# Second expert products with w2 as weights: 256 tokens moved, the result turned and brought back through DRAM

## The chip, the cores and the metric

The kernel runs on one core of a Trainium2 chip. The metric is the device time of one execution in microseconds. The kernel before was run three times; the median is 2457.13 us (2457.12 to 2459.16).

Engines are named as in the profile: PE is TensorE's matmuls and PEld its weight loads, DVE is VectorE, ACT ScalarE, POOL GpSimd, SP SyncE. A name with a q, such as SPq, is the engine's instruction queue, which also issues DMA transfers. All data are 32-bit floats.

## The reference

```python
# attention: u, v (8, 2496, 256), z (8, 2496, 64)
scores = (1.0 / S) * np.matmul(z, z.transpose(0, 2, 1))
attn = np.maximum(scores, 0.0) ** 2
x = (u * np.matmul(attn, v)).reshape(19968, 256)
# experts: w1 (8, 256, 1024), w2 (8, 1024, 256)
expert_idx = token_ids * np.int64(2654435761) % np.int64(8)
for e in range(8):
    mask = expert_idx == e
    h = np.maximum(x[mask] @ w1[e], 0.0)
    out[mask] = h @ w2[e]
```

## The kernel before

The first part computes the attention, and beside it sorts the tokens by expert: each row of x is scattered to a slot in DRAM (`x_slots`), so that tokens of one expert lie together. The second part works through the slots in 40 big blocks (`NL`) of 512 tokens, each with one expert, and one small block of 128.

A big block has two layers. Both are done by a scheme of Strassen's kind: each operand is split into four quarters, and seven products of sums of quarters take the place of eight. `products` (L929) writes down the order of the seven (1, 6, 7, 5, 2, 3, 4) and what is added to what, and yields after each. Products 1 and 5 stay in a PSUM bank of the tag "held" (two banks), since products 2 and 3 are added to them in place; 6, 7 and 4 pass through the tag "other". The second layer has only one "other" bank, so product 7 can't be written before VectorE has added product 6 to product 1 (`ro`, L935), and product 4 not before product 7 is read.

- `up_big` (L955) is the first layer: w1 quarters are the weights, 256 tokens are moved at a time, and the hidden features lie on the partitions. It goes through the seven products twice, two slices of hidden features at a time: 14 steps, called U. A step is four matmuls of 256 columns. A 32-bit matmul shows as two records in the profile, so a step has 8 records.
- `down_big` (L987) is the second layer: the hidden values of 128 tokens are the weights, and 128 output features of w2 are moved, so that the result has tokens on the partitions, as rows. It has seven steps, called D, of 8 matmuls of 128 columns (16 records) each. VectorE and ScalarE put the results into `o_sb` (two buffers); when the rows of two 128-token tiles are complete, `store` (L921) has GpSimd scatter them to the output by an indirect DMA.

What is done when is written out by hand: `tc.manual_schedule()` keeps every engine's instructions in the order in which the program issues them. The outer loop (L1056) has 41 iterations. Iteration i takes the U steps of block i, the D steps of block i-1, and the two X steps of block i+1 (`turn_x`, L742: X1 turns the loaded tokens by VectorE's transposes of 32x32 squares, L752; X2 makes their sums, L757 to L760). A string gives the order:

```python
    ORDER = {"first": "UUUUGUUUGUUUUUUU", "second": "DUDUDUUDUUDUU" "XUxUDUXUDUUUU",
             "other": "UuUDUuUXDUdUDU" "UDUDUxUDUXUDU", "end": "DDDDDDDd"}
```

Small letters belong to the small block and are empty until the last but one iteration. An iteration of the kind "other" is therefore U1 U2 D1 U3 U4 X1 D2 U5 U6 D3 U7 U8 D4 U9 D5 U10 U11 D6 U12 X2 U13 D7 U14; D1, D2, D3 are products 1, 6, 7, and D7 is product 4.

At the end of iteration i, SyncE's queue gets the loads in this order:

```python
        for j in at(i + 2):
            load_x(j)
        for m in range(2):
            for j in at(i + 2 - m):
                load_w(j, m)
```

`load_x` (L735) loads a block's tokens into `xq` by four DMAs of 128 KB, in pieces of 256 B; it has two buffers, and the buffer for block i+2 is free once block i is turned, in iteration i-1. `load_w` (L763) loads w1 or w2 with the quarter sums prepared earlier (1792 KB each, in pieces of 14336 B per partition); w1 of block i+2 needs the buffer of block i, free after the last U step of iteration i. So SyncE's queue waits at the weights until an iteration's end, issues them, and then issues the next block's `xq` at once, an iteration early.

The quarters of w2 and their sums are prepared in the attention part (`prepare`, L678) and addressed by `w2_block` (L714). With the output features split in two, a quarter's columns are either contiguous halves or, after the change, every second column.

The attention part has transfers of the same form as the ones of the change: after each tile of queries, four DMAs write `x_sb` to DRAM (`put`, L364; 4 x 128 KB in pieces of 256 B), and the rows are fetched again (L372, L223; pieces of 1 KB).

Of the kernel before, what the change touches and what calls it, by code (L numbers as in the profile page):

```python
# [10 lines left out]
F32 = mybir.dt.float32  # L11
# [13 lines left out]
def kernel(  # L25
# [10 lines left out]
    nc = tc.nc  # L36

    B, S, D = u.shape
    K = z.shape[-1]
    N = B * S  # L40
    E, _, F = moe_w1.shape
# [3 lines left out]
    P = 128  # L45
    L = 32
    DP = D // P
    FP = F // P
# [6 lines left out]
    BLK = 512  # L55
    TB = BLK // P
    NL = E * -(-N // (E * BLK))
# [84 lines left out]
    FQ = FP // 2  # L142
# [565 lines left out]
            nc.gpsimd.dma_start(out=w_dram[e, m], in_=w[:].rearrange("p i f -> p (i f)"))  # L708


    def w1_block(w, i):
        return w[:, i]

    def w2_block(w, i):  # L714
        if i < 4:
            return w[:, 0:4].rearrange("p i f -> p (i f)").rearrange("p (c f i d) -> p c i f d", c=2, f=FQ, i=2)[:, i // 2, i % 2]
        return w[:, i].rearrange("p (f d) -> p f d", f=FQ)


# [2 lines left out]
    w1, w2, xq, xT, hid = {}, {}, {}, {}, {}  # L722

    def big(j):
        return j < NL
# [6 lines left out]
    def half(j):  # L732
        return len(slot_tiles(j)) * P // 2
# [29 lines left out]
    def load_w(j, m):  # L763

        e = nc.sync.value_load(eb_i[0:1, j:j + 1], min_val=0, max_val=E - 1)
        if big(j):
            w = (w2pool if m else wpool).tile([P, 7, HF], F32, name="w")
            nc.sync.dma_start(w[:].rearrange("p i f -> p (i f)"), w_dram[ds(e, 1), m].rearrange("one p f -> (one p) f"))
        elif m == 0:
            w = w2pool.tile([P, DP, F], F32, name="w1s")  # L770
            nc.sync.dma_start(
                w[:], moe_w1[ds(e, 1)].rearrange("one d f -> (one d) f").rearrange("(c p) f -> p c f", p=P))
        else:
            w = w2pool.tile([P, FP, D], F32, name="w2s")
            nc.sync.dma_start(
                w[:], moe_w2[ds(e, 1)].rearrange("one f d -> (one f) d").rearrange("(c p) d -> p c d", p=P))
        (w1, w2)[m][j] = w
# [52 lines left out]
    for i, (b, g, s) in enumerate(steps):  # L830
# [54 lines left out]
        elif is_routed:  # L885
            if fetched and i >= fetched[0][0] + (5 if i < len(steps) - NT else 2):
                rows = fetched.pop(0)[1]
# [33 lines left out]
    def store(j, t, o):  # L921
        col = slot_tiles(j)[t]
        st = nc.gpsimd.indirect_dma_start(  # L923
            out=out[:], out_offset=bass.IndirectOffsetOnAxis(ap=idx[:, col:col + 1], axis=0),
            in_=o, in_offset=None, bounds_check=N - 1, oob_is_err=False)
        tc.declare_no_dep(st.ins, group="rows", reason="each token has its own row")
        tc.add_to_no_dep_group("rows", st.ins)

    def products(made, p1, u, c11, c12, c21, c22, done):  # L929


        ps1 = made(1, None)
        nc.scalar.copy(p1, ps1)
        yield
        nc.vector.tensor_add(u, p1, made(6, None))  # L935
        yield
        ps7 = made(7, None)
        yield
        ps5 = made(5, None)
        nc.vector.tensor_add(c21, u, ps7)  # L940
        nc.vector.tensor_add(c22, c21, ps5)  # L941
        done(c22, 1, 1)
        yield
        made(2, ps1)
        done(c11, 0, 0, ps1)
        yield
        made(3, ps5)
        nc.vector.tensor_add(c12, u, ps5)
        done(c12, 0, 1)
        yield  # L950
        nc.vector.tensor_sub(c21, c21, made(4, None))
        done(c21, 1, 0)
        yield
# [30 lines left out]
            nc.vector.tensor_sub(x21, x11, x21)  # L984
            nc.vector.tensor_sub(s4, x12, s2)

    def down_big(j):  # L987
        h, sums = hid[j]
        n = half(j) // P
        x11, x12, x21, x22 = (h[:, k, i] for i in range(2) for k in range(2))  # L990
        s1, s2, s4 = (sums[:, i] for i in range(3))
        take = {1: (x11, 0), 2: (x12, 2), 3: (s4, 3), 4: (x22, 6), 5: (s1, 4), 6: (s2, 5), 7: (x21, 1)}

        def made(m, ps):
            first = ps is None
            if first:
                held = m in (1, 5)
                ps = down_ps.tile([P, 2, P], F32, name="o_ps", tag="held" if held else "other", bufs=2 if held else 1)[:, 0:n]
            x, k = take[m]
            for t in range(n):  # L1000
                for f in range(FQ):
                    nc.tensor.matmul(ps[:, t], x[:, f, ts(t, P)], w2_block(w2[j], k)[:, f], start=first and t == 0 and f == 0,  # L1002
                                     stop=f == FQ - 1, skip_group_check=True)
            return ps
        r = rpool.tile([P, 2, 2, P], F32, name="ro")[:, :, 0:n]
        o = rpool.tile([P, TB, D], F32, name="o_sb")
        c = lambda i, k: o[:, ts(i, n), ts(k, P)]

        def done(x, i, k, ps=None):
            if ps is not None:  # L1010
                nc.scalar.copy(x, ps)
            elif i != k:
                for t in range(i * n, i * n + n):
                    store(j, t, o[:, t, :])
        yield from products(made, r[:, 0], r[:, 1], c(0, 0), c(0, 1), c(1, 0), c(1, 1), done)

    def up_small(j):
        x = xT[j][0]
# [37 lines left out]
    for i in range(NL + 1):  # L1056
        parts = {}
        for j in at(i):
            parts["U" if big(j) else "u"] = (up_big if big(j) else up_small)(j)
        for j in at(i - 1):  # L1060
            parts["D" if big(j) else "d"] = (down_big if big(j) else down_small)(j)
        for j in at(i + 1):
            if i:
                parts["X" if big(j) else "x"] = turn_x(j)
        if i == 0:
            x_sb = late.tile([P, 2, 2, D], F32, name="x_row")
            parts["G"] = gate_at_once(*done, x_sb, lambda: down_ps.tile([P, 2, D], F32, name="g_ps", tag="held", bufs=2))
        for p in ORDER["first" if i == 0 else "second" if i == 1 else "end" if i == NL else "other"]:
            next(parts.get(p, iter(())), None)
        for p in parts.values():  # L1070
            assert next(p, None) is None and next(p, "end") == "end"
        if i == 0:
            for k in range(4):
                sort(*done[:2], x_sb, k)
            closing["late"].close()
            w2pool = pool("w2pool", 2, reuse_waits="tile")
            load_w(0, 1)
# [5 lines that stand above are left out]
# [4 lines left out]
    n_others = nc.values_load(others_i[0:1, 0:1], min_val=0, max_val=NR - SMALLS)  # L1087
    with tc.For_i(0, n_others, 1) as n:
        e = nc.sync.value_load(eb_i[0:1, ds(n + NL + SMALLS, 1)], min_val=0, max_val=E - 1)
        w1s = w2pool.tile([P, DP, F], F32, name="w1s")  # L1090
        nc.sync.dma_start(w1s[:], moe_w1[ds(e, 1)].rearrange("one d f -> (one d) f").rearrange("(c p) f -> p c f", p=P))
        w2s = w2pool.tile([P, FP, D], F32, name="w2s")
        nc.sync.dma_start(w2s[:], moe_w2[ds(e, 1)].rearrange("one f d -> (one f) d").rearrange("(c p) d -> p c d", p=P))
        x_in = gpool.tile([P, P // L, DP, L], F32, name="xqs")
        src = x_dram[ds((n + NL * TB + SMALLS) * P, P), :].rearrange("(j r) (i e) -> i r j e", r=L, e=DL)
        for i in range(P // L):
            nc.sync.dma_start(out=x_in[ts(i, L)].rearrange("r j h k -> r j (h k)"), in_=src[i])
        to = rpool.tile([P, 1], I32, name="to")
        nc.sync.dma_start(out=to[:], in_=slot_dram[:].rearrange("(p c) -> p c", p=P)[:, ds(n + NL * TB + SMALLS, 1)])
        x = gpool.tile([P, 1, DP, P], F32, name="xTs")  # L1100
        nc.vector.transpose(x[:, 0].rearrange("p h (j r) -> p j h r", r=L), x_in[:])
        h = hpool.tile([P, FP, P], F32, name="h1")
        for f in range(0, FP, 4):
            ps = down_ps.tile([P, 4, P], F32, name="h_ps", tag="any")
            for i in range(4):
                for c in range(DP):
                    nc.tensor.matmul(ps[:, i, :], w1s[:, c, ts(f + i, P)], x[:, 0, c], start=(c == 0), stop=(c == DP - 1))
            nc.vector.tensor_scalar_max(h[:, f:f + 4], ps[:], 0.0)
        ps = down_ps.tile([P, D], F32, name="o_ps", tag="any")
        for f in range(FP):  # L1110
            nc.tensor.matmul(ps[:], h[:, f], w2s[:, f, :], start=(f == 0), stop=(f == FP - 1))
        o = rpool.tile([P, D], F32, name="o1")
        nc.scalar.copy(o[:], ps[:])
        nc.gpsimd.indirect_dma_start(
            out=out[:], out_offset=bass.IndirectOffsetOnAxis(ap=to[:, 0:1], axis=0),
            in_=o[:], in_offset=None, bounds_check=N - 1, oob_is_err=False)
# [28 lines left out]
```

## Time and profile before

| what | value |
|---|---|
| median of 3 runs | 2457.13 us |
| the profiled execution's own time | 2461.1 us |
| its span, first to last instruction | 2459.3 us |
| mean granted TensorE clock | 0.998 |
| HBM read, written | 332.83 MB, 179.81 MB |
| matmul and weight-load records of L1002 (D steps) | 4480 each |
| mean duration of a record: 128 columns (L1002), 256 columns (L971) | 275 ns, 380 ns |

[...] The busy share of an engine is over the whole span; the two parts have different limits. The expert stage runs from about 1450 us to the end, one block in 24.59 us.

### The profile page before, as it was taken

What the parts mean: (1) busy time and instruction counts of PE and PEld (TensorE: products, weight loads), DVE (VectorE), ACT (ScalarE), POOL (GpSimd) and SP (SyncE); (2) the same over time, 40 slices, a digit from 0 to 9 for tenths busy, and PEclk for the clock granted to TensorE, in tenths of its full rate; (3) what the DMA queues carried; (4) which work ended last, traced back from release to release, by engine and by line L of the source; (5) the groups of instructions that cost most, each with busy time, mean ns of one, the idle gap of its engine ahead of it and who ended that gap; (6) DMA issues with size and microseconds to landing.
All of it is one profiled execution on the core that took longest, in us unless ns stands there. A gap on an engine that the chain in (4) does not pass through costs nothing.

```text
span 2459.3 us, 36675 instructions
## 1 busy us (share of the span) xinstructions
PE 2435.6 (99%) x13351; PEld 2075.4 (84%) x13351; DVE 1767.7 (72%) x3655; ACT 728.5 (30%) x1210; POOL 570.9 (23%) x547
## 2 busy tenths in 40 slices
PE   8999999999999999999999999999999999999998
PEld 6787787787787787787787789999999999999997
DVE  7778778868868769778778666666666666666663
ACT  4324314324224224224233212222222222222221
POOL 0002013423524424423321021111111111121112
PEclk9999999999999999999999999999999999999999
DMA  7866667888888788878778686565656565656562
GB/s 150 202 201 188 163 191 235 241 270 249 249 257 254 253 244 254 253 217 248 259 214 248 196 236 192 186 199 187 198 188 197 188 197 187 197 187 199 187 208 73
DMA packets 412104, 518.94 MB, mean 211 GB/s; under 512 B 254252, under 2 KB 347261, under 8 KB 393488
## 3 DMA queue, kind: packets, MB, share of 16 engines
q1 hardware_dynamic: 350704, 326.23, 47.4%
q10 hardware_dynamic: 32448, 97.86, 12.0%
q0 software_dynamic: 28768, 92.49, 10.4%
q8 instruction: 105, 1.72, 0.3%
q14 instruction: 79, 0.65, 0.1%
HBM read 332.83 MB, written 179.81 MB: 208 GB/s over the span
## 4 chain that ended last, share of the span: by engine, by line
PE 94%; DMA 2%; issue 2%; DVE 1%; SPq 1%; ACT 0%; ACTq 0%; POOL 0%; another core or an unknown queue 0%; DVEq 0%; POOLq 0%
PE acc L326 45%; PE o_ps L1002 20%; PE h_ps L971 20%; PE s_ps L251 9%; DMA v_sb<-in_v_dram 1%; DMA zT<-zT 0%; DMA x<-x_sb 0%; SPq L303 0%; ACT a L255 0%; DMA a<-scores 0%; DVE t L275 0%; DMA zn<-in_z_dram 0%; POOL out_dram L923 0%; PE h_ps L1025 0%; SPq L364 0%
## 5 line engine op out<-in xcount | busy, mean ns | idle before, releaser
L255 ACT ACTIVATE a<-s_ps 128x512 f32<-128x512 f32 (+1 forms) x480 | 246.7, 599 | 703.4 <-PE s_ps L251 586.8
L326 PE MATMUL acc<-t,vc 128*128 128x256 f32 (+3 forms) x1600 | 402.2, 373 | 0.0
L326 PEld LDWEIGHTS acc<-a,v_sb 128*128 128x128 f32 (+1 forms) x1600 | 293.2, 190 | 119.1 <-issue 53.1
L326 PE MATMUL acc<-a,v_sb 128*128 128x256 f32 (+3 forms) x1600 | 382.7, 382 | 0.1
L326 PE MATMUL acc<-t,v_sb 128*128 128x256 f32 (+3 forms) x1600 | 369.7, 373 | 0.0
L923 POOL DMA_INDIRECT out_dram<-o_sb,idx x160 | 162.3, 1014 | 822.6 <-issue 774.8
L411 POOL DMA_INDIRECT x_slots<-x_row,row x160 | 192.8, 1205 | 685.6 <-DVE x_row L389 510.8
L326 PEld LDWEIGHTS acc<-t,vc 128*128 128x128 f32 (+1 forms) x1600 | 303.5, 190 | 33.6
L326 PEld LDWEIGHTS acc<-t,v_sb 128*128 128x128 f32 (+1 forms) x1600 | 303.4, 190 | 33.7
L1002 PEld LDWEIGHTS o_ps<-w,h 128*128 128x128 f32 x2560 | 311.4, 192 | 9.1 <-DVE ro L935 0.8
L971 PE MATMUL h_ps<-xs,w 128*128 128x256 f32 x1280 | 316.6, 380 | 0.0
L1002 PE MATMUL o_ps<-w,h 128*128 128x128 f32 x2560 | 312.2, 275 | 0.6 <-DVE ro L935 0.6
L275 DVE TENSOR_TENSOR t<-a 128x512 f32<-128x512 f32 (+1 forms) x200 | 134.3, 671 | 206.2 <-ACT a L264 147.5
L978 ACT ACTIVATE h<-h 128x512 f32<-128x512 f32 x240 | 151.4, 631 | 413.4 <-DVE h L941 177.6
L251 PE MATMUL s_ps<-zT 64*128 64x512 f32 (+1 forms) x960 | 242.8, 619 | 9.7 <-DVE zT L186 6.9
L971 PEld LDWEIGHTS h_ps<-xs,w 128*128 128x128 f32 x1280 | 228.8, 191 | 23.1
L1002 PEld LDWEIGHTS o_ps<-w,hs 128*128 128x128 f32 x1920 | 233.1, 192 | 6.1
L971 PE MATMUL h_ps<-xT,w 128*128 128x256 f32 x960 | 234.5, 380 | 3.1 <-DVE h L941 3.1
L1002 PE MATMUL o_ps<-w,hs 128*128 128x128 f32 x1920 | 233.8, 275 | 0.0
L291 DVE STREAM_TRANSPOSE mirror<-a 128x256 f32<-128x256 f32 x640 | 217.7, 406 | 0.6 <-DMA scores<-mirror 0.6
L662 POOL DMA_INDIRECT slot_tokens<-token,addr x160 | 170.6, 1066 | 134.1 <-DVE addr L650 85.7
L326 PE MATMUL acc<-a,vc 128*128 128x256 f32 (+3 forms) x800 | 201.1, 373 | 0.0
(169 smaller groups left out, 2384.0 us busy)
## 6 DMA issues: line engine op xcount, KB each, us to landing
w<-w_blocks SPq DMA_DIRECT2D x80, 1792.0 KB
scores<-mirror SPq DMA_DIRECT2D x192, 256.0 KB
a<-scores ACTq DMA_DIRECT2D x48, 1024.0 KB
scores<-mirror SPq DMA_DIRECT2D x224, 128.0 KB
a<-scores ACTq DMA_DIRECT2D x32, 896.0 KB
w_blocks<-w POOLq DMA_DIRECT2D x16, 1792.0 KB
xq<-x_slots SPq DMA_DIRECT2D x160, 128.0 KB
u_sb<-in_u_dram SPq DMA_DIRECT2D x72, 256.0 KB
```

The source lines that it names most:

```text
L251: nc.tensor.matmul(flat(ps)[:, 0:2 * w].rearrange("p (q c) -> p q c", q=2), tile_of_keys(b, h, s, j), q_h, start=True, stop=True)
L255: nc.scalar.activation(of[:, :, j, h].rearrange("p m q e -> p q m e"), flat(ps)[:, 0:2 * w].rearrange("p (q m e) -> p q m e", q=2, e=in_bl ...
L275: nc.vector.tensor_sub(t1, y12, y11)
L291: nc.vector.transpose(to, in_blocks(a, g)[:, :, j, h].rearrange("p i q (r t) -> p t i q r", t=2)[:, t])
L326: nc.tensor.matmul(acc[k][:, half, 0:w], x[0:n, j, :], y[0:n, j], start=(first and j == 0 and half == 0), stop=(last and j == 1), skip_gro ...
L411: st = nc.gpsimd.indirect_dma_start(out=x_dram[:, :], out_offset=bass.IndirectOffsetOnAxis(ap=row[0:m, c:c + 1], axis=0), in_=x_sb[0:m, q, ...
L662: st = nc.gpsimd.indirect_dma_start(out=slot_dram[:, None], out_offset=bass.IndirectOffsetOnAxis(ap=addr[0:n, to:to + 1], axis=0), in_=tok ...
L923: st = nc.gpsimd.indirect_dma_start(out=out[:], out_offset=bass.IndirectOffsetOnAxis(ap=idx[:, col:col + 1], axis=0), in_=o, in_offset=Non ...
L971: nc.tensor.matmul(ps[:, r], w1[j][:, k, ts(f + r, P)], y, start=first and r == 0, stop=True, skip_group_check=True)
L978: lambda o, i, k, ps=None: nc.scalar.activation(o, o if ps is None else ps, AF.Relu))
L1002: nc.tensor.matmul(ps[:, t], x[:, f, ts(t, P)], w2_block(w2[j], k)[:, f], start=first and t == 0 and f == 0, stop=f == FQ - 1, skip_group_ ...
```

## The change

In the second layer, blocks 0 to 38 now take w2 as the weights and move 256 tokens, the form of the first layer. A D step is then 4 matmuls of 256 columns (8 records). The result (`oT`) has output features on the partitions. VectorE turns it by 32x32 squares into `y` (two transposes after product 3, two after product 4). After the block's last step, SyncE writes `y` to a tensor in DRAM by four DMAs in pieces of 256 B, GpSimd fetches the rows into `o_sb` (now one buffer) by one DMA, and then issues the four stores. These follow the `yield from`, so they are issued when the iteration's string is through, before the iteration's `load_x` and `load_w`. In `y` two output features lie next to each other that come from the two halves of the split; so the split of w2's columns is now by odd and even columns (`w2_block`). Block 39 keeps the old form (`down_last`), with the new split and the single `o_sb` buffer.

```diff
     def w2_block(w, i):
         if i < 4:
-            return ....rearrange("p (c f i d) -> p c i f d", c=2, f=FQ, i=2)[:, i // 2, i % 2]
+            return ....rearrange("p (c f d i) -> p c i f d", c=2, f=FQ, i=2)[:, i // 2, i % 2]
...
+    def down_bank(m, banks):
+        first = {2: 1, 3: 5}.get(m, m)
+        if first == m:
+            held = m in (1, 5)
+            banks[m] = down_ps.tile([P, 2 * P], F32, name="o_ps", tag="held" if held else "other", bufs=2 if held else 1)
+        return banks[first], first == m
...
     def down_big(j):
...
-        def made(m, ps):
...
-            for t in range(n):
-                for f in range(FQ):
-                    nc.tensor.matmul(ps[:, t], x[:, f, ts(t, P)], w2_block(w2[j], k)[:, f], ...)
-        r = rpool.tile([P, 2, 2, P], F32, name="ro")[:, :, 0:n]
-        o = rpool.tile([P, TB, D], F32, name="o_sb")
-        c = lambda i, k: o[:, ts(i, n), ts(k, P)]
+        def made(m, _):
+            ps, first = down_bank(m, banks)
+            x, k = take[m]
+            for f in range(FQ):
+                nc.tensor.matmul(ps[:], w2_block(w2[j], k)[:, f], x[:, f], ...)
+            return ps[:]
+        r = rpool.tile([P, 2, 2 * P], F32, name="ro")
+        o = rpool.tile([P, 2, 2, 2 * P], F32, name="oT")
+        y = rpool.tile([P, BLK // L, L, 2], F32, name="y", bufs=1)
+        c = lambda i, k: o[:, k, i]
 
         def done(x, i, k, ps=None):
             if ps is not None:
                 nc.scalar.copy(x, ps)
             elif i != k:
-                for t in range(i * n, i * n + n):
-                    store(j, t, o[:, t, :])
+                for k in range(2):
+                    nc.vector.transpose(y[:, ts(i, BLK // L // 2), :, k], o[:, k, i].rearrange("p (j r) -> p j r", r=L))
         yield from products(made, ...)
+        rows = nc.dram_tensor(f"o_{j}", (BLK, D), F32)
+        for q in range(P // L):
+            nc.sync.dma_start(out=rows.rearrange("(j r) (q e) -> q r j e", r=L, q=P // L)[q], in_=y[ts(q, L)].rearrange("r j d k -> r j (d k)"))
+        y = rpool.tile([P, TB, D], F32, name="o_sb", bufs=1)
+        nc.gpsimd.dma_start(out=y[:], in_=rows.rearrange("(t p) d -> p t d", p=P))
+        for t in range(TB):
+            store(j, t, y[:, t, :])
...
+    def down_last(j):
...
+        o = rpool.tile([P, TB, D], F32, name="o_sb", bufs=1)
+        c = lambda i, k: o[:, ts(i, n)].rearrange("p t (d k) -> p t d k", k=2)[:, :, :, k]
```

The tiles `w1s` and `w2s` of the small block get one buffer each instead of two, and the loop picks `down_last` for block 39.

More of the change, by code (lines that the diff above doesn't have):

```diff
@@ L715, in w2_block @@
         if i < 4:
-            return w[:, 0:4].rearrange("p i f -> p (i f)").rearrange("p (c f i d) -> p c i f d", c=2, f=FQ, i=2)[:, i // 2, i % 2]
+            return w[:, 0:4].rearrange("p i f -> p (i f)").rearrange("p (c f d i) -> p c i f d", c=2, f=FQ, i=2)[:, i // 2, i % 2]
         return w[:, i].rearrange("p (f d) -> p f d", f=FQ)
@@ L769, in load_w @@
         elif m == 0:
-            w = w2pool.tile([P, DP, F], F32, name="w1s")
+            w = w2pool.tile([P, DP, F], F32, name="w1s", bufs=1)
             nc.sync.dma_start(
@@ L773, in load_w @@
         else:
-            w = w2pool.tile([P, FP, D], F32, name="w2s")
+            w = w2pool.tile([P, FP, D], F32, name="w2s", bufs=1)
             nc.sync.dma_start(
@@ L985, in up_big, with down_factors @@
             nc.vector.tensor_sub(s4, x12, s2)
-    def down_big(j):
+    def down_factors(j):
         h, sums = hid[j]
-        n = half(j) // P
         x11, x12, x21, x22 = (h[:, k, i] for i in range(2) for k in range(2))
         s1, s2, s4 = (sums[:, i] for i in range(3))
-        take = {1: (x11, 0), 2: (x12, 2), 3: (s4, 3), 4: (x22, 6), 5: (s1, 4), 6: (s2, 5), 7: (x21, 1)}
-        def made(m, ps):
[L995 to L998, printed above, removed]
+        return {1: (x11, 0), 2: (x12, 2), 3: (s4, 3), 4: (x22, 6), 5: (s1, 4), 6: (s2, 5), 7: (x21, 1)}
@@ new lines, in down_bank, with down_big, done @@
+    def down_bank(m, banks):
[4 more added lines that the diff above has]
+        return banks[first], first == m
+    def down_big(j):
+        take, banks = down_factors(j), {}
+        def made(m, _):
+            ps, first = down_bank(m, banks)
+            x, k = take[m]
+            for f in range(FQ):
+                nc.tensor.matmul(ps[:], w2_block(w2[j], k)[:, f], x[:, f], start=first and f == 0, stop=f == FQ - 1, skip_group_check=True)
+            return ps[:]
[3 more added lines that the diff above has]
+        c = lambda i, k: o[:, k, i]
+        def done(x, i, k, ps=None):
+            if ps is not None:
+                nc.scalar.copy(x, ps)
+            elif i != k:
+                for k in range(2):
+                    nc.vector.transpose(y[:, ts(i, BLK // L // 2), :, k], o[:, k, i].rearrange("p (j r) -> p j r", r=L))
+        yield from products(made, r[:, 0], r[:, 1], c(0, 0), c(0, 1), c(1, 0), c(1, 1), done)
+        rows = nc.dram_tensor(f"o_{j}", (BLK, D), F32)
[5 more added lines that the diff above has]
+            store(j, t, y[:, t, :])
@@ L999, in made @@
+    def down_last(j):
+        take, banks = down_factors(j), {}
+        n = TB // 2
+        def made(m, _):
+            ps, first = down_bank(m, banks)
             x, k = take[m]
@@ L1001, in made @@
                 for f in range(FQ):
-                    nc.tensor.matmul(ps[:, t], x[:, f, ts(t, P)], w2_block(w2[j], k)[:, f], start=first and t == 0 and f == 0,
+                    nc.tensor.matmul(ps[:, ts(t, P)], x[:, f, ts(t, P)], w2_block(w2[j], k)[:, f], start=first and t == 0 and f == 0,
                                      stop=f == FQ - 1, skip_group_check=True)
-            return ps
-        r = rpool.tile([P, 2, 2, P], F32, name="ro")[:, :, 0:n]
-        o = rpool.tile([P, TB, D], F32, name="o_sb")
-        c = lambda i, k: o[:, ts(i, n), ts(k, P)]
+            return parts(ps[:])
+        parts = lambda x: x.rearrange("p (t d) -> p t d", t=n)
+        r = rpool.tile([P, 2, 2 * P], F32, name="ro")
+        o = rpool.tile([P, TB, D], F32, name="o_sb", bufs=1)
+        c = lambda i, k: o[:, ts(i, n)].rearrange("p t (d k) -> p t d k", k=2)[:, :, :, k]
         def done(x, i, k, ps=None):
@@ L1014, in done @@
                     store(j, t, o[:, t, :])
-        yield from products(made, r[:, 0], r[:, 1], c(0, 0), c(0, 1), c(1, 0), c(1, 1), done)
+        yield from products(made, parts(r[:, 0]), parts(r[:, 1]), c(0, 0), c(0, 1), c(1, 0), c(1, 1), done)
     def up_small(j):
@@ L1060 @@
         for j in at(i - 1):
-            parts["D" if big(j) else "d"] = (down_big if big(j) else down_small)(j)
+            parts["D" if big(j) else "d"] = (down_small if not big(j) else down_last if j == NL - 1 else down_big)(j)
         for j in at(i + 1):
@@ L1089 @@
         e = nc.sync.value_load(eb_i[0:1, ds(n + NL + SMALLS, 1)], min_val=0, max_val=E - 1)
-        w1s = w2pool.tile([P, DP, F], F32, name="w1s")
+        w1s = w2pool.tile([P, DP, F], F32, name="w1s", bufs=1)
         nc.sync.dma_start(w1s[:], moe_w1[ds(e, 1)].rearrange("one d f -> (one d) f").rearrange("(c p) f -> p c f", p=P))
-        w2s = w2pool.tile([P, FP, D], F32, name="w2s")
+        w2s = w2pool.tile([P, FP, D], F32, name="w2s", bufs=1)
         nc.sync.dma_start(w2s[:], moe_w2[ds(e, 1)].rearrange("one f d -> (one f) d").rearrange("(c p) d -> p c d", p=P))
```

## The prediction

> **What bounds the kernel now.** I read the page's busy times and its chain first.
>
> ```profile
> PE 2435.6 (99%) x13351; PEld 2075.4 (84%) x13351; DVE 1767.7 (72%) x3655; ACT 728.5 (30%) x1210; POOL 570.9 (23%) x547
> PE 94%; DMA 2%; issue 2%; DVE 1%; SPq 1%; ACT 0%; ACTq 0%; POOL 0%; another core or an unknown queue 0%; DVEq 0%; POOLq 0%
> ```
>
> TensorE is the end-setting engine: time comes out only where its work shrinks, and any wait that reaches it goes in whole. So I took one block of the expert stage, first TensorE (PE), in the timeline from the start of block iteration T0 = 1912.00:
>
> ```profile
> 1912.00 1.03 PE L971 MATMUL h_ps<-xT,w 128*128 128x256 f32 x4
> 1912.86 1.03 PE L971 MATMUL h_ps<-xs,w 128*128 128x256 f32 x4
> 1913.73 1.95 PE L1002 MATMUL o_ps<-w,h 128*128 128x128 f32 x16
> 1915.51 1.89 PE L971 MATMUL h_ps<-xs,w 128*128 128x256 f32 x8
> 1917.24 1.95 PE L1002 MATMUL o_ps<-w,hs 128*128 128x128 f32 x16
> 1919.02 1.89 PE L971 MATMUL h_ps<-xT,w 128*128 128x256 f32 x8
> 1920.75 1.95 PE L1002 MATMUL o_ps<-w,h 128*128 128x128 f32 x16
> ```
>
> Starts are what count (ends are modelled). A D step (16 records of 128 columns) takes 1.78 us, two U steps (8 records of 256) 1.73, with no gap. Next VectorE (DVE) in the same stretch:
>
> ```profile
> 1911.33 0.42 DVE L951 TENSOR_TENSOR o_sb<-o_sb,o_ps 128x256 f32<-128x256 f32 x1 [1.03 <-PE o_ps L1002]
> ...
> 1917.44 0.69 DVE L941 TENSOR_TENSOR h<-h,h_ps 128x512 f32<-128x512 f32 x1 [0.18 <-PE h_ps L971]
> 1918.05 1.30 DVE L752 STREAM_TRANSPOSE xT<-xq 128x512 f32<-128x512 f32 x2
> 1919.29 0.42 DVE L935 TENSOR_TENSOR ro<-ro,o_ps 128x256 f32<-128x256 f32 x1
> ```
>
> The first line is the last work on the block's outputs. The third turns the next block's tokens; behind it stands `ro`, which empties the single "other" bank that D3 (1920.75) has to write. Then SyncE's queue (SP), here and where the expert stage begins:
>
> ```profile
> 1433.87 6.04 SPq L740 DMA_DIRECT2D xq<-x_slots  x8
> ...
> 1912.19 1.49 SPq L768 DMA_DIRECT2D w<-w_blocks  x2
> 1913.79 8.30 SPq L740 DMA_DIRECT2D xq<-x_slots  x4
> ```
>
> The four `xq` loads go out right behind the two weight loads and are used a whole iteration later. Last, busy time by stretch (columns: us, PE, PEld, DVE, ACT, POOL, granted clock, DMA share, GB/s):
>
> ```profile
> 1887.60:1888.60 1.00, 1.00 (x6) 0.87 (x5) 0.99 (x2) 0.27 (x1) 0.81 (x1) 1.00 0.16 43
> 1888.60:1898.40 9.80, 9.80 (x71) 9.26 (x70) 6.43 (x11) 3.06 (x6) 1.03 (x1) 1.00 1.00 384
> 1898.40:1902.40 4.00, 4.00 (x28) 3.74 (x27) 3.36 (x6) 1.10 (x2) 0.00 (x0) 1.00 1.02 171
> 1902.40:1909.00 6.60, 6.60 (x48) 6.24 (x47) 3.74 (x9) 1.32 (x3) 0.00 (x0) 1.00 0.01 2
> 612.00:615.00 3.00, 3.00 (x15) 1.72 (x12) 3.00 (x11) 2.21 (x5) 0.43 (x1) 1.00 0.96 211
> 1435.20:1441.60 6.40, 6.40 (x36) 6.37 (x35) 6.01 (x14) 0.00 (x0) 0.00 (x0) 1.00 1.13 179
> ```
>
> The weights were issued at 1887.60 and their bytes start 1.0 us later; they fill the DMA engines for 9.8 us. The four `xq` loads, in pieces of 256 B, run some 4 us at 171 GB/s; then the engines rest 6.6 us. The last two rows are other transfers in 256 B pieces: the attention part's writes of `x_sb` (L364) and the eight `xq` loads of 1433.87.
>
> **The change, part by part.** *TensorE's saving.* Seven D steps in each of 39 blocks go from 16 records of 128 columns to 8 of 256. The U steps are that very form. 1.783 us (the iteration of 24.59 less 14 x 0.865, by 7) less 1.730 is 0.053 us a step: 39 x 7 x 0.053 = 14.5 us off. Half the weight loads go, but they already lie under the matmuls, so that is all. Four of the seven weights are now read with a stride of two; the score products (L251) also load mostly stride-two weights, and their loads' mean (192 ns) is that of L1002's (192), so I add nothing; were it to cost as much as it saves, the 14.5 would be gone (rival 3).
>
> *VectorE.* Four transposes of 128x256 a block: the row of that size (L291, `mirror`) has 217.7 us busy over 640, 0.34 each, so 1.4 us in an iteration in which VectorE works 16.2 of 24.6. They lie beside TensorE; only the last two matter, as they end the block's `y`: 1911.33 + 0.42 + 0.34 + 0.41 = 1912.50, that is T0 + 0.5. The adds keep their size (0.42). The sums prepared from w2 in the attention part read with stride two, 32 instructions in all, where VectorE has 1% of the chain: nothing.
>
> *SyncE's queue, the costly part.* The four writes of `y` to DRAM are issued after the block's last step, ahead of `xq`(i+2), w1(i+2) and w2(i+1). Their wait is for the transposes at the iteration's end, so SyncE sits in it, and `xq`(i+2), which used to be issued at T0 + 1.8 of the iteration before, is now queued behind: it goes out only after T0 + 0.5 of the very iteration that turns it. 37 iterations are so (i = 1 to 37, turned in 2 to 38).
>
> When must it be there? X1 starts at T0 + 6.05 now. From X1's start to `ro`'s end are 1919.71 - 1918.05 = 1.66 us; D3 starts at T0 + 8.75, less 0.11 for two shorter D steps: 8.64. So the tokens may be late until T0 + 7.0; past that TensorE waits at D3, microsecond for microsecond, and nothing later gives it back, since TensorE has no gaps to absorb it.
>
> When is it there? T0 + 0.5, plus 1.0 from issue to the first bytes, plus two times 0.524 MB in 256 B pieces. By the quickest rows: 2.5 us (211 GB/s) and 3.1 (171), landing at T0 + 7.1, a stall of 0.1. By the row most like it (eight such transfers back to back on this queue: 1.05 MB, 6.4 us at 179 GB/s and a tail of up to 1 us): T0 + 7.9 to 8.9. On top comes the gather: GpSimd waits for the writes, issues (0.6 us, L708), and its 0.52 MB run among the tail of `xq`: at the 302 GB/s of the 1 KB rows fetched at 518.5 to 520.5, 1.7 us, of which 0 to all falls in front of the last token. T0 + 7.9 to 10.6, and 11.5 with the 0.9 us by which the `xq` stretch of 4.0 outlasts its bytes at 171 GB/s. I take 9.2 (8.5 and 0.7), nearest to the eight-transfer row: a stall of 2.2 us. 37 x 2.2 = 81 us; between 4 (0.1) and 167 (4.5).
>
> [...] The writes at 612 to 615 run at 211 GB/s, no slower than the reads at 171, so I go by the row.
>
> *The weight loads* follow `xq`: issued by about T0 + 6, they take 9.8 us behind it and are there by T0 + 20, with w1 wanted at T0 + 24: hidden by 4 us, more if the iteration lengthens. *GpSimd's queue*: gather at about T0 + 5, four stores (1.28 us apart) behind its landing, all done before T0 + 17; the single `o_sb` and `y` are free an iteration later: hidden.
>
> *The end.* Block 39 keeps its form, but its first write to `o_sb` (2438.58, T0 + 6.55 with T0 = 2432.03) must now wait for block 38's stores: `y` T0 + 0.5, bytes 1.0 + 3.0, gather 0.6 + 1.0 + 1.8, four stores to T0 + 12.8, their reads some 1.5 later: T0 + 14.3. D6 (2441.95, T0 + 9.92) needs the second add after it (0.7 later): T0 + 15.1, so 5 us late; 2 to 9 as the transfers go.
>
> *Sum:* -14.5 + 81 + 5 = +72 us on the profiled execution (2461.1, of it 2459.3 span), which stands 4.0 above the median. On the median of 2457.1: 2529.
>
> **Rivals.** (1) *The tokens arrive in time.* For it: the DMA engines rest from 1902.4 to 1909, so the volume fits, and by the quickest rows the stall is 0.1 us. Against: these rows leave out the tail and the gather. It decides at a landing of T0 + 7.0 (up to 7.3, where stall and saving balance); then -14.5 + 4 = about -10: 2447, faster. 0.10.
>
> (2) *The stall is far longer.* Gather, stores and tokens meet in the DMA engines, the slowest of 16 sets the landing, and w1 gets late too: landing T0 + 12 or more, stall 5: 37 x 5 - 14.5 + 7 = +178: 2635. For it: the `xq` stretch outlasts its bytes even now, with the engines to itself. Against: 6.6 us of rest per iteration. 0.13. The granted clock is 1.00 in all the rows above, where TensorE never rests. [...]
>
> (3) *The saving is not there* (stride-two weights load slower, D steps as long as before) while the stall is as forecast: 2529 + 14.5 = 2544. 0.05.
>
> **How the numbers follow.** The forecast has 0.72. The range reaches from a landing at T0 + 7.7 (37 x 0.7 - 14.5 + 3 = +14) rounded down to 2465, to one at about 11.3 (37 x 4.3 - 14.5 + 7 = +152) at 2610: it holds (3) and most of the forecast, and leaves out (1) and most of (2). A difference under 0.2% (4.9 us) can't be told from none. Faster: 0.09, nearly all of (1); within 0.2%: 0.04, the thin strip at 7.2 to 7.4; slower: 0.87.
>
> **What would show it.** Right: in the windows of an iteration 256 B traffic first, from T0 + 1.5, the weights after; iterations of 26 to 27 us; the wait list with VectorE's transpose of `xq` held by the DMA of `xq`, some 3 us each and 37 times, and PE's D steps held by `ro`; D steps of 1.73 us start to start. Wrong: no idle PE in front of D3 (rival 1); iterations of 29 us or more or waits for `w` (rival 2); D steps still of 1.78 (rival 3).

## The result, and the profile after

The changed kernel takes 2520.89 us (median of 4 runs, 2518.17 to 2527.66), the kernel before 2458.14 us (4 runs, 2457.12 to 2462.95). The ratio is 1.0255, with an interval of 1.023 to 1.0281: slower by some 63 us, where 72 was forecast. The profiled execution of the changed kernel took 2522.63 us, with a span of 2520.4.

The page's busy times and its chain of the changed kernel:

```profile
PE 2431.8 (96%) x11167; PEld 2009.7 (80%) x11167; DVE 1816.4 (72%) x3811; ACT 728.3 (29%) x1210; POOL 601.7 (24%) x586
PE 81%; SPq 6%; DMA 6%; DVE 4%; issue 2%; POOL 0%; DVEq 0%; POOLq 0%; ACTq 0%
```

TensorE has 2184 records fewer and is busy 3.8 us less, but of the chain it holds 81% now, not 94%. What came in is SyncE's queue, transfers and VectorE. The chain by line names them: the loads of `xq` 5%, the writes of `y` (L1027) 3%, the `xq` issues (L741) 3%.

TensorE's timeline over the iteration that begins at T0 = 1932.22 (start, duration, engine, line, operation; in brackets the idle time before and who ended it):

```profile
1932.22 1.03 PE L972 MATMUL h_ps<-xT,w 128*128 128x256 f32 x4
1933.08 1.03 PE L972 MATMUL h_ps<-xs,w 128*128 128x256 f32 x4
1933.94 1.89 PE L1011 MATMUL o_ps<-h,w 128*128 128x256 f32 x8
1935.67 1.89 PE L972 MATMUL h_ps<-xs,w 128*128 128x256 f32 x8
1937.40 1.89 PE L1011 MATMUL o_ps<-hs,w 128*128 128x256 f32 x8
1939.12 1.89 PE L972 MATMUL h_ps<-xT,w 128*128 128x256 f32 x8
1942.52 2.00 PE L1011 MATMUL o_ps<-h,w 128*128 128x256 f32 x8 [1.50 <-DVE ro L936]
...
1958.17 1.03 PE L972 MATMUL h_ps<-xT,w 128*128 128x256 f32 x4
```

A D step is now 1.73 us from start to start (1933.94 to 1935.67), as a pair of U steps is. (A U step is two matmuls, four records, and not the four matmuls and eight records given above; the 14 steps of 40 blocks make 2240 records. A pair of them has the records of one D step.) In front of D3 there is a gap: the pair U5, U6 starts at 1939.12, and D3 3.40 us later, 1.67 more than a step. (The bracket says 1.50, as it counts from the modelled end of the last matmul.) The whole iteration takes 25.95 us.

The same stretch on VectorE and on SyncE's queue:

```profile
1932.01 0.77 DVE L1023 STREAM_TRANSPOSE y<-oT 128x256 f32<-128x256 f32 x2
...
1940.85 1.30 DVE L753 STREAM_TRANSPOSE xT<-xq 128x512 f32<-128x512 f32 x2 [2.56 <-DMA xq<-x_slots]
1942.08 0.38 DVE L936 TENSOR_TENSOR ro<-ro,o_ps 128x256 f32<-128x256 f32 x1
```

```profile
1932.81 2.20 SPq L1027 DMA_DIRECT2D o<-y  x4
1935.05 2.58 SPq L741 DMA_DIRECT2D xq<-x_slots  x4
1938.45 1.51 SPq L769 DMA_DIRECT2D w<-w_blocks  x2
```

This is the whole story in six lines. The result is turned at 1932.0, the writes go out as soon as that is done (1932.81), the `xq` loads behind them, and VectorE stands for 2.56 us at the turning of tokens that have not landed. `ro`, queued behind that, empties D3's bank at 1942.08 + 0.38; D3 starts at 1942.52.

Waits of the expert stage (1450 to 2520 us: total, times, longest), one line of VectorE and two of TensorE:

```profile
DVE xT L753 <- DMA xq<-x_slots: 95.9, 37, 4.6
...
PE o_ps L1011 <- DVE ro L936: 57.3, 37, 3.5
...
PE o_ps L1043 <- DVE o_sb L942: 7.5, 1, 7.5
```

37 waits of TensorE at D3, for the 37 blocks whose `xq` is queued behind `y`; by starts they are 63.3 us, 1.7 each. Then one of 7.5 at the last block.

Busy time by stretch in that iteration (us, PE, PEld, DVE, ACT, POOL, clock, DMA share, GB/s), and two stretches of the end:

```profile
1932.81:1933.67 0.86, 0.86 (x6) 0.76 (x5) 0.86 (x2) 0.28 (x1) 0.00 (x0) 1.00 0.00 0
1933.67:1940.85 7.18, 7.18 (x35) 6.16 (x33) 4.15 (x7) 2.42 (x5) 0.79 (x1) 1.00 0.89 180
1940.85:1950.50 9.65, 8.15 (x38) 7.15 (x38) 6.75 (x12) 1.73 (x3) 1.99 (x2) 1.00 0.99 410
1950.50:1958.76 8.26, 8.26 (x40) 7.33 (x39) 5.70 (x14) 2.23 (x4) 2.24 (x3) 1.00 0.19 66
...
2497.00:2500.16 3.16, 0.00 (x1) 0.00 (x1) 0.84 (x2) 0.39 (x1) 0.22 (x1) 0.65 0.12 42
2500.16:2503.74 3.58, 3.58 (x17) 3.58 (x18) 0.00 (x0) 0.00 (x0) 0.00 (x0) 0.50 0.01 2
```

First bytes 0.86 us after the issue; then 7.18 us at 180 GB/s, nearly all small pieces (their packets, 1.05 MB, run for 6.25 us, to 1939.92, and the first of the weights follow); then the weights; then near rest. The order of before (weights, then tokens, then rest) is turned round, and over the iteration as a whole the DMA engines still have time to spare (0.19 busy in its last 8 us). The last two rows belong to the end, whose timeline on VectorE and TensorE is:

```profile
2499.15 0.42 DVE L941 TENSOR_TENSOR o_sb<-ro,o_ps 128x256 f32<-128x256 f32 x1 [12.24 <-DMA out_dram<-o_sb,idx]
```

```profile
2500.16 3.78 PE L1043 MATMUL o_ps<-w,hs 128*128 128x128 f32 x16 [7.51 <-DVE o_sb L942]
2503.74 2.43 PE L1043 MATMUL o_ps<-w,h 128*128 128x128 f32 x16
```

Block 39's first write to `o_sb` waits for the stores of block 38, TensorE stands idle for 7.5 us in front of D6, and D6 then takes 3.58 us where a step of this form takes 1.78, at a granted clock of 0.50.

Where the time went, between the two profiled executions: the first U step starts at 1451.1 us in both, so the attention part is as it was. From there to the start of the last U step: 980.1 before, 1030.3 after, +50.2. From that step to the end of the span: 28.1 before, 39.0 after, +10.9. Together +61.1, the difference of the spans (2520.4 less 2459.3).

### The profile page after: what moved, and what is told of

The parts are those of the page before. It is cut to its first block, busy times and chain, and to the rows that moved or that the text cites. A ratio compares the mean times of both kernels' runs of the same rounds, so it can differ in the third digit from the quotient of the medians.

```text
span 2520.4 us, 32665 instructions
## 1 busy us (share of the span) xinstructions
PE 2431.8 (96%) x11167; PEld 2009.7 (80%) x11167; DVE 1816.4 (72%) x3811; ACT 728.3 (29%) x1210; POOL 601.7 (24%) x586
## 4 chain that ended last, share of the span: by engine, by line
PE 81%; SPq 6%; DMA 6%; DVE 4%; issue 2%; POOL 0%; DVEq 0%; POOLq 0%; ACTq 0%
PE acc L326 48%; PE o_ps L1011 14%; PE h_ps L972 10%; PE s_ps L251 9%; DMA xq<-x_slots 5%; SPq L1027 3%; SPq L741 3%; DVE y L1023 1%; DVE xT L753 1%; DVE oT L952 1%; DVE ro L936 0%; DMA zT<-zT 0%; POOL out_dram L924 0%; SPq L166 0%; PE o_ps L1043 0%
## 5 line engine op out<-in xcount | busy, mean ns | idle before, releaser
L1011 PE MATMUL o_ps<-h,w 128*128 128x256 f32 x1248 | 300.6, 384 | 57.3 <-DVE ro L936 57.3
L1011 PEld LDWEIGHTS o_ps<-h,w 128*128 128x128 f32 x1248 | 241.0, 195 | 98.1 <-DVE ro L936 72.1
L972 PEld LDWEIGHTS h_ps<-xs,w 128*128 128x128 f32 x1280 | 243.2, 190 | 32.3
L1011 PE MATMUL o_ps<-hs,w 128*128 128x256 f32 x936 | 221.1, 379 | 0.0
L972 PEld LDWEIGHTS h_ps<-xT,w 128*128 128x128 f32 x960 | 182.2, 190 | 27.4 <-DVE h L942 2.9
```

The source lines that it names most:

```text
L972: nc.tensor.matmul(ps[:, r], w1[j][:, k, ts(f + r, P)], y, start=first and r == 0, stop=True, skip_group_check=True)
L1011: nc.tensor.matmul(ps[:], w2_block(w2[j], k)[:, f], x[:, f], start=first and f == 0, stop=f == FQ - 1, skip_group_check=True)
```

## Experiments

The theory (Q in the texts on record) is the order in SyncE's queue: the new writes wait for the end of an iteration, and the next block's `xq` stands behind them. Its rivals put the gap in front of D3 on the new work itself, wherever it is queued: on VectorE's four transposes, or on the load of the DMA engines by writes, gather and late stores. The runs are told in the order in which they argue.

### Tokens ahead of the writes

```diff
+        for j in at(i + 2) if i else []:
+            load_x(j)
         for p in parts.values():
             assert next(p, None) is None and next(p, "end") == "end"
...
-        for j in at(i + 2):
+        for j in at(i + 2) if not i else []:
             load_x(j)
```

The second line lets the generators run out, and with that issues the four writes; the four `load_x` issues now stand ahead of them. Nothing else is different: same transposes, writes, gather and stores.

> The changed kernel with one edit of order: from iteration 1 on, the next-but-one block's four xq loads are put on SyncE's queue ahead of the four writes of y instead of behind them. Theory Q (the tokens stand behind the writes in SyncE's queue, and D3 waits for them): xq is again issued an iteration early, VectorE's wait for xq (95.9 us in the changed kernel) and TensorE's wait for ro (57.3 us, some 63 by starts) vanish, and 2520.9 - 63 = 2458 us; the late end of the last block (11 us) stays. Rival V (VectorE's four more transposes a block push ro, whatever the tokens do): the wait for ro stays, 2521. Rival M (1 MB more of traffic a block slows the tokens and weights in the DMA engines in any order): a good part of the wait stays, 2480 to 2500.

Measured: 2452.77 us (2450.0 to 2454.96) against 2457.82 of the kernel before, ratio 0.9974 (0.9965 to 0.9983). SyncE's queue over more than an iteration, and the one line that is left of TensorE's two lines in the waits of the changed kernel:

```profile
1905.48 1.50 SPq L769 DMA_DIRECT2D w<-w_blocks  x2
1907.03 8.58 SPq L741 DMA_DIRECT2D xq<-x_slots  x4
...
1926.35 2.17 SPq L1027 DMA_DIRECT2D o<-y  x4
1929.64 1.51 SPq L769 DMA_DIRECT2D w<-w_blocks  x2
```

```profile
PE o_ps L1043 <- DVE o_sb L942: 7.4, 1, 7.4
```

`xq` goes out behind the weights again, at 1907, and the writes come at 1926 with nothing behind them that is due soon. All 37 waits at D3 are gone; the iteration takes 24.17 us. So 68 us of the changed kernel are the order of the queue, 5 more than was expected from the 63 us of waits: D3 itself is longer behind a stall, 5.8 us in sum (see the account of the prediction). The transposes, the bytes and the late stores are all still there, and cost TensorE nothing in these blocks: both rivals fall.

### The steps alone

```diff
-        y = rpool.tile([P, BLK // L, L, 2], F32, name="y", bufs=1)
...
-                    nc.vector.transpose(y[:, ts(i, BLK // L // 2), :, k], ...)
+                    store(j, 2 * i + k, o[:, k, i])
         yield from products(made, ...)
-        rows = nc.dram_tensor(f"o_{j}", (BLK, D), F32)
...
-            store(j, t, y[:, t, :])
```

> The changed kernel without the way back to rows: no transposes, no y, no writes, no gather; the four stores take oT as it is, at the steps where the kernel before stored. What is stored is not turned, so only the time counts. It keeps the D steps of 256 columns with w2 (every second column) as the weights. Theories Q and V alike: the saving by itself, 39 x 7 x 0.053 = 14.5 us, 2457.5 - 14.5 = 2443, and no wait of TensorE for ro. Rival S (stride-two weights or the wider steps cost what they save): 2457. The last block's single o_sb buffer waits for nothing here.

Measured: 2439.57 us (2438.84 to 2441.51), ratio 0.9922 (0.9907 to 0.9937): 18 us faster than before. TensorE's timeline:

```profile
1901.35 1.89 PE L1011 MATMUL o_ps<-h,w 128*128 128x256 f32 x8
1903.08 1.89 PE L972 MATMUL h_ps<-xs,w 128*128 128x256 f32 x8
1904.81 1.89 PE L1011 MATMUL o_ps<-hs,w 128*128 128x256 f32 x8
```

D steps of 1.73 us, no gap, an iteration of 24.17 instead of 24.59: 0.42 x 39 = 16.4 us, and 17.3 from the first to the last U step. The saving is there, and weights with a stride of two cost TensorE nothing that this can tell.

### The last block with a buffer of its own

```diff
     def down_last(j):
...
-        o = rpool.tile([P, TB, D], F32, name="o_sb", bufs=1)
+        o = rpool.tile([P, 2, 2, 2 * P], F32, name="oT")[:].rearrange("p a b x -> p (a b x)").rearrange("p (t d) -> p t d", d=D)
```

> The changed kernel with one edit at the end: block 39 collects its rows in a tile of the name oT (two buffers) instead of the single o_sb, so that its first add does not wait for block 38's stores. Theory (the late end is this wait, 7.5 us of TensorE, and the slower clock behind it): from the last U step to the end of the span 27 to 29 us instead of 38.3, and 2520.9 - 10 = 2511. Rival G (the end is late since block 38's stores now stand in front of block 39's in GpSimd's queue): the end stays at 36 to 38 us, 2519 to 2521. The 37 stalls at D3 stay in both.

Measured: 2517.31 us (2509.76 to 2526.76), ratio 1.0234 (1.021 to 1.0259). By the time alone this is inconclusive: the median is 3.6 below the changed kernel's, and the runs spread over 17 us. In the traced run the expert stage happens to begin 5 us later than in that of the changed kernel (first U step at 1456.2 us, not 1451.1), which hides most of the gain. The trace decides the point it was made for: the wait for `o_sb` is gone, and from the start of the last U step to the end are 30.9 us instead of 39.0 (2 us over the 27 to 29 of the theory, far from rival G's 36 to 38), while the waits at D3 stay:

```profile
PE o_ps L1011 <- DVE ro L936: 55.5, 37, 3.7
```

So the end's 8.1 us hang on the one `o_sb` buffer, which block 39 shares with the gather of block 38.

### Both repairs

This is the first experiment's edit and the third's together.

> Both edits at once: the xq loads ahead of the writes of y, and block 39's rows in a tile of its own. Theory Q: no wait of TensorE for ro in the big blocks, the end 27 to 30 us after the last U step instead of 38.6, so 2452.8 - 9 = 2444 (2441 to 2448), against 2439.6 of the D steps alone: the way back through DRAM then costs some 4 us. If the DMA traffic itself still cost something, iterations would be longer than the 24.17 us of the D steps alone.

Measured: 2444.33 us (2443.57 to 2450.63) against 2458.06 of the kernel before, ratio 0.994 (0.9925 to 0.9954). Windows of one whole iteration:

```profile
1905.00:1929.17 24.17, 24.17 (x114) 21.48 (x113) 17.46 (x34) 6.67 (x12) 5.15 (x6) 1.00 0.79 241
```

TensorE never rests, with the DMA engines at 0.79. This version beats both kernels, by 14 us and by 77. The way of the result back through DRAM then costs about 5 us (2444.33 less 2439.57 of the steps alone), of which the profile shows 2.5 at the end (30.7 us after the last U step instead of 28.2). From the first U step to the last the two traces are equal (962.9 and 962.8 us); the rest of the 5 is not assigned. The first U step comes anywhere from 1447 to 1456 us in the nine traces, so 2 or 3 us between medians say little.

### The writes alone

The kernel before, with four writes in pieces of 256 B added at the end of a block's second layer:

```diff
         yield from products(made, ...)
+        if j < NL - 1:
+            rows = nc.dram_tensor(f"o_{j}", (BLK, D), F32)
+            for q in range(P // L):
+                nc.sync.dma_start(out=rows.rearrange("(j r) (q e) -> q r j e", r=L, q=P // L)[q], in_=o[ts(q, L)].rearrange("r t (a e) -> r (t a) e", e=D // 4))
```

> The kernel before with only the four DMA writes of 256 B pieces added, at the place and on the queue where the change has them: they copy the block's finished o_sb to a tensor in DRAM that nobody reads (its content is of no use; the output is as before). No transposes, no gather, D steps of 128 columns. Theory Q: the writes are issued when the last add is done, some 0.2 us before T0; by the changed kernel's 8.0 us from the first write's issue to X1 the tokens are turned from T0 + 7.8, and D3 (here at T0 + 8.75) allows T0 + 7.1: a stall of 0.7 us in 37 iterations, 26 us, so 2484 (2470 to 2500), with waits of TensorE for ro. Rival V: no transposes, so nothing is added, 2457. Rival M: half of the traffic of the change in engines that rest 6.6 us an iteration, 2457.

Measured: 2545.81 us (2542.32 to 2557.02), ratio 1.0354 (1.0334 to 1.0374). The direction is right, the size is a miss: +88 us instead of +26. (The traced execution is the slowest of the five, 2557.02.) GpSimd's and SyncE's timelines and TensorE's at D3 in one iteration:

```profile
1901.84 0.97 POOL L923 DMA_INDIRECT out_dram<-o_sb,idx  x1 [0.65 <-DVE o_sb L951]
1903.12 1.03 POOL L923 DMA_INDIRECT out_dram<-o_sb,idx  x1 [0.30 <-issue]
```

```profile
1901.63 2.27 SPq L1019 DMA_DIRECT2D o<-o_sb  x4
1903.94 3.66 SPq L740 DMA_DIRECT2D xq<-x_slots  x4
```

```profile
1908.84 1.89 PE L971 MATMUL h_ps<-xT,w 128*128 128x256 f32 x8
1913.40 3.51 PE L1002 MATMUL o_ps<-w,h 128*128 128x128 f32 x16 [2.67 <-DVE ro L935]
1916.71 1.25 PE L971 MATMUL h_ps<-xs,w 128*128 128x256 f32 x4
```

Here the block's own stores go out in the same moment as the writes (1901.84 and 1903.12), and their bytes are taken to run among them; in the changed kernel the stores come 15 us later. X1 starts 9.2 us (median) after the first write's issue, not 8.0. And after some of the stalls D3 takes 3.31 us from start to start, not 1.78.

### The writes alone, stores later

To test that reading, the same kernel with a gather into a buffer of its own and the four stores behind it, as the changed kernel has them (the small block's weights get one buffer each, to make room):

```diff
-                for t in range(i * n, i * n + n):
+                for t in range(i * n, i * n + n) if j == NL - 1 else ():
                     store(j, t, o[:, t, :])
...
+            o2 = rpool.tile([P, TB, D], F32, name="o_2", bufs=1)
+            nc.gpsimd.dma_start(out=o2[:], in_=rows.rearrange("(t p) d -> p t d", p=P))
+            for t in range(TB):
+                store(j, t, o2[:, t, :])
```

> The kernel before (D steps of 128 columns, no transposes) with everything else of the change: the four writes from o_sb, GpSimd's gather, and the four stores behind the gather, so that no store runs beside the writes and xq. The rows come out in another order, so only the time counts. It tells why e2 took 88 us where 26 were expected. Theory: in e2 the stores of the same block (1904 to 1907) ran in the DMA engines between the writes and xq and put the tokens off by 2 us more, and with it the stall over the length that brings the half clock. Then here the tokens are turned 8.0 us after the first write's issue as in the changed kernel: a stall of 0.7 us, 37 x 0.7 = 26, so 2484 (2470 to 2500), with no half clock but at the end. Otherwise (something in the D steps of 128 columns or the reading of o_sb makes the writes slow): 2540 to 2550 as in e2.

Measured: 2501.59 us (2497.46 to 2504.78), ratio 1.0172 (1.0154 to 1.019). Half of the 88 us is gone, though the time is still 1.6 over the upper end of what was expected. X1 starts 8.0 us (median) after the writes' issue, the number of the changed kernel. TensorE's waits at D3, first in the writes alone, then with the stores later:

```profile
PE o_ps L1002 <- DVE ro L935: 72.2, 38, 3.9
```

```profile
PE o_ps L1002 <- DVE ro L935: 29.9, 38, 3.0
```

So the stores beside the writes made most of the miss, 44 of 62 us. What is left above the expectation: by starts the stalls are 35 us, not 26, among them those of five iterations in which X1 comes 9.2 to 10.5 us after the issue (why these are late was not settled); D3 behind the stalls is 5.8 us longer in sum, two of the stalls having brought lengthened steps (D3 2.76 us from start to start at 1911.38, the U step behind it 1.65), where a half clock was expected only at the end; and the end is 2 us later.

### The writes twice

```diff
+        again = nc.dram_tensor(f"again_{j}", (BLK, D), F32)
+        for q in range(P // L):
+            nc.sync.dma_start(out=again.rearrange("(j r) (q e) -> q r j e", r=L, q=P // L)[q], in_=y[ts(q, L)].rearrange("r j d k -> r j (d k)"))
         y = rpool.tile([P, TB, D], F32, name="o_sb", bufs=1)
```

> The changed kernel with the four writes of y made twice (the second four to a tensor that nobody reads), both ahead of xq on SyncE's queue. Theory Q: xq lands later by what 0.52 MB in 256 B pieces take, 2.5 to 2.9 us, and TensorE's stall at D3 grows by as much: 37 x 2.7 = 100 us, so 2621; the stalls, then of 4 to 4.5 us, are also long enough for the half clock of 3.4 us that e2 showed behind stalls of 2.7 us and more, up to 37 x 1.7 = 63 us on top: 2621 to 2684. If the landing of xq were set by something else than the writes ahead of it (the reads themselves, the gather), little would change: 2521 to 2540.

Measured: 2821.74 us (2818.52 to 2825.46), ratio 1.147 (1.1449 to 1.1492). The doubled transfer is paid where the theory says, in front of D3, but at far more than its own length, and 2621 to 2684 is missed by 138 us: X1 starts 14.3 us after the first issue instead of 8.0, and TensorE's waits and one D3 read

```profile
PE o_ps L1011 <- DVE ro L936: 283.1, 37, 9.5
```

```profile
2022.30 3.78 PE L1011 MATMUL o_ps<-h,w 128*128 128x256 f32 x8 [7.65 <-DVE ro L936]
2025.88 1.48 PE L972 MATMUL h_ps<-xs,w 128*128 128x256 f32 x4
```

Two things come together. With `xq` issued 2.8 us later, the gather's 0.52 MB run ahead of most of `xq` (gather from about 2013.4 to 2015.5, `xq` mostly from 2015), where in the changed kernel they run behind it. That would make some 5 of the 6.3 us by which X1 comes later; the rest is not assigned. And in every iteration the stall, of 6.4 to 9.5 us, is followed by a D3 of 3.2 to 3.6 us instead of 1.73, and mostly by a lengthened U7 too (1.48 us above, as against 1.03). 283 - 57 = 226 us of stall, 61 of longer D3 steps than in the changed kernel (66.7 less 5.8) and 15 of the two U steps behind D3 make 302, and the kernel is 301 us above the changed one. This is the long stall of the prediction's second rival, brought about by 0.52 MB more in the queue.

## Why the prediction was right, step by step

- *TensorE's saving*, 14.5 us by 0.053 a step: the steps alone gave 18 by the medians and 16.4 to 17.3 by the trace. Right, 2 to 4 us too small. Rival 3 (no saving) is refuted by that run.
- *VectorE:* the last two transposes take 0.77 us, the writes go out at T0 + 0.6. Forecast was T0 + 0.5. That the transposes cost nothing else is shown by the first experiment.
- *The deadline*, T0 + 7.0: with X1 at T0 + 8.63 it gives a stall of 1.63; 1.67 was there. This step, made from the trace of before alone, held to 0.05 us.
- *The landing*, taken at T0 + 9.2: X1 came at T0 + 8.6, within the eight-transfer row's bounds of 7.9 to 8.9. The 0.7 us set aside for the gather were not paid: it is issued at 1937.95, 5.7 us after T0, and nearly all its packets come behind the tokens. So the stall was 1.7 instead of 2.2, 63 us instead of 81. This is the term that was mis-sized most, by 18 us. The twofold writes show that the gather's share is not always nothing: there its packets ran for some 2 us ahead of most of the tokens.
- *Weights and GpSimd's queue:* no wait of TensorE for `w` is listed; the stores end at T0 + 21 rather than 17, still hidden.
- *The end*, 5 us (2 to 9): 10.9. The add came at T0 + 16.9 instead of 14.3 and D6 at T0 + 17.9 instead of 15.1, since writes and gather each took about a microsecond longer; that alone would have been within the bounds. What the prediction had not put into this term at all is the half clock behind a stall of 7.5 us: 1.8 us in D6 and 0.5 in D7.
- *Rival 1* (tokens in time) did not occur; the first experiment shows what it pays, -5 us on the medians for -10. *Rival 2* did not occur, as nothing fell in between writes and tokens.
- *The sum* on the profiled execution: from the first U step to the last, -18.9 (961.2 us in the trace of the first experiment, which has no stall at D3, instead of 980.1) + 63.3 + 5.8 = 50.2, as measured; with 10.9 at the end, 61.1. The 5.8 stood in no term of the prediction: behind a stall D3 itself takes 1.84 us instead of 1.73 in 36 iterations (its first weight load then starts with it, not 0.2 us ahead), and 3.5 us, at half clock, behind the one longest stall. (It is -18.9, and not the -17.3 of the steps alone, because the trace of before has 3.4 us of half clock behind a stall of 2.50 us at the start of the expert stage, and that of the steps alone lengthened steps in the same place: the two U steps from 1461.10 take 1.87 and 1.54 us. The traces of the changed kernel and of the first experiment have that stall, too, but the two U steps behind it take 0.97 and 0.86 us in both.)
- *Right, and in part by luck.* The mechanism and its place are as forecast, and the time lies well inside the range. But the 72 came within 9 us of the 63 because errors cancel: the stall was taken 18 us too long and the saving 3 to 4 us too small, while the end and the longer D3 steps together came 12 us higher.

Two assumptions stand behind the terms of the prediction. *Writes in pieces of 256 B at the rate of such reads:* the stretch of 7.18 us carried 180 GB/s, with 0.52 MB of writes of 256 B in it, against 179 in the stretch of the eight reads of before (the 256 B pieces alone, writes and reads, made 168 in their 6.25 us). So the choice of that row held. *A granted clock of 1.00 throughout:* behind the long waits it was 0.50 (7.51 us in front of the matmuls of 2500.16 in the changed kernel, 7.65 in front of those of 2022.30 in the writes twice), and behind some of the shorter ones too, as the last section tells.

## What to carry to other kernels

A transfer that waits for work at the end of an iteration must not stand in a queue ahead of one that waits for nothing: here four issues in the wrong place cost 68 us, and moving them made the same kernel 5 us faster than before. Price such an insertion by the deadline of what stands behind it (here T0 + 7.0, read from the first engine that blocks on it), not by the share of time in which the DMA engines rest. Where a buffer count is cut, look at the one block that is treated differently: the last block's shared `o_sb` cost 8 us in a single place.

## What the runs showed of the hardware

*A stall of some 2.5 us was followed by a half clock in some places and not in others.* In the writes alone, the stall of the iteration shown above and D3 after it, by windows (columns as above):

```profile
1911.60:1913.40 1.80, 0.00 (x0) 0.00 (x1) 1.66 (x4) 0.00 (x0) 0.00 (x0) 1.00 1.04 446
1913.40:1916.70 3.30, 3.30 (x16) 3.30 (x17) 0.54 (x1) 0.63 (x1) 0.00 (x0) 0.55 1.02 433
```

An idle time of 2.67 us by the bracket (2.83 when counted from start to start, 4.56 less the 1.73 of the two U steps) was followed by 3.3 us at a mean clock of 0.55. D3 took 3.31 us instead of 1.78 and the U step behind it 1.08 instead of 0.86, so that the stall cost 4.6 us in all. But the wait of 2.50 us at the start of the expert stage, which the kernel before and the changed kernel share, went both ways: before, the matmuls behind it start at 1465.82, and the clock is 0.50 from 1466.48 to 1469.88; in the changed kernel they start at 1464.96, and the clock is 1.00 from 1461.44 to 1470.00. Of the 37 stalls at D3 in the changed kernel, 1.7 us each on average, half clock followed one, the longest (3.50 us by the bracket, in front of the matmuls of 2255.52; 0.50 from 2255.58 to 2258.98). The mean granted clock of the profiled executions was 0.998 before, 0.997 in the changed kernel, 0.991 in the writes alone and 0.948 in the writes twice. So stalls of like length can cost quite differently; what decides between them was not shown.

*The order among queues shifts with a few microseconds.* The same gather ran behind the tokens in the changed kernel, where their issue began 2.9 us before its own (1935.05, 1937.95), and ahead of most of them in the doubled writes, where both began together (2011.49, 2011.61) and the second four writes still ran before the tokens; by the length of the gather's packets (2013.4 to 2015.5) this was worth an estimated 2 us an iteration.
